# B of two head pairs loaded from ScalarE's and GpSimd's queues instead of SyncE's, with some factor copies moved on ScalarE

## The chip, the cores and the metric

The kernel runs on one core of a Trainium2 chip. The metric is the device time of one execution in microseconds (us). The kernel before takes 122.59 us, the median of three runs (122.33 to 122.97).

## The reference

Two layers follow each other. The first is a scan in chunks (a state-space layer): 4 batches, 8 heads, 768 tokens, head width 32, state width 16. In words: with `cum` the running sum of log(a) inside a chunk,

```
M        = (C @ B.T) * exp(cum_i - cum_j), causal
y        = M @ x + (C @ state) * exp(cum)
state    = exp(sum(la)) * state + (B * exp(cum_last - cum)).T @ x
```

The second is a bilinear feed-forward layer on the heads put side by side (3072 tokens, width 256, inner width 1536): `out = ((y @ w_a) * (y @ w_b)) @ w_out`.

## The kernel before, in words

The sequence is cut into 6 blocks of 128 tokens. A block has two pairs of batches, so there are 12 pairs: pairs 0 and 1 are block 0, pairs 2 and 3 block 1, pairs 4 and 5 block 2. The order of the work is written out by hand: on each engine and on each DMA queue the instructions stand in the order of the program text.

What is computed for a pair:

- **Scaled B and C.** The decay is put on B and C as factors. `batch_factors` (L301) copies the factors from a turned tile `Pt` to `FC`, one copy for each batch, and `batch_inverse` (L309) takes the reciprocal on VectorE to get `FB`. `scale_q` (L341) multiplies C and B of a pair by them on GpSimd into a tile `planes`; its inputs `cq` and `bq` come in four DMAs each for a block (`load_q`, L160, one DMA for each batch). `turn` (L353) transposes `planes` on VectorE, and `scores` (L398) multiplies them on TensorE into the four banks `SC`.
- **Masks.** `mask` (L442) multiplies the scores by the causal table, on VectorE, or by way of a ScalarE copy `tmp` on GpSimd.
- **State.** B is needed a second time with tokens on the partitions, as `bn` (two DMAs for each of the pairs 2 and 3, `load1` at L143, DMA line L153). `scale_bc` (L324, line L333) scales it on GpSimd to `bm`, which `outputs` (L532) multiplies with x. The pairs 2 and 3 take x in fp32 by SyncE (`load_x32`, L721) and ScalarE casts it at L725.
- **Feed-forward.** For block 0 a `unit` (L626) is a pair p and a number k2: `unit_mm` (L593, line L598) makes four matmuls with `Wa` into a bank `aps` and four with `Wb` into a bank `bps`; ScalarE copies `aps` to `asb` (L612), and VectorE multiplies `bps` by `asb` into `hk` (`times`, L622). `out_mm` (L637) multiplies `hk` with `Wo`. From block 1 on, `bunit` (L659, lines L667 and L679) and `bout` (L693, L705) do the same for a whole block.

PSUM has eight banks. Four are the scores' `SC`; the other four are given out in turn by `bank` (L129), which takes the next digit of the string `BANKS`. A matmul that writes a bank waits until its last user has been read. So `BANKS` decides on whom TensorE waits.

Around the change (all in the part that starts at 20 us): the units (0,3), (0,4) and (1,3) are done together: three times `Wa`, three ScalarE copies, then three times `Wb` with `times` behind each on VectorE. `turn(2)` stands on VectorE after `times` of (0,4) and ahead of `times` of (1,3). Then come the unit (0,5), the matmuls of unit (1,4), `scores(2)`, `turn(3)`, the masks of pair 2, unit (1,5), the first halves of `out_mm`, `scores(3)`, the masks of pair 3, `outputs(1)`, and block 1's feed-forward. `turn(4)` and `scores(4)` of block 2 stand after four `bunit`s of block 1.

Each DMA of the queues of SyncE and ScalarE adds to one of eight counters in turn, and an instruction that uses a counter again first waits until the DMA before it on that counter has landed. DMAs of GpSimd's queue have eight counters of their own.

Of the kernel before, what the change touches and what calls it, by code (L numbers as in the profile page):

```python
# [19 lines left out]
SS = 64.0  # L20

BANKS = (
    "012313213212301230123012302103120312301230132013210320132012301230132103210321023013201320"
    "1321023102310231021302130213021302130213021302310231023102310231023102310231023102310"
)


# [1 line left out]
def kernel(  # L29
# [13 lines left out]
    nc = tc.nc  # L43

    nb, H, S, D = x.shape
# [14 lines left out]
    NT = NBLK - PJ // NBP  # L60
# [72 lines left out]
    def tiles(p):  # L133
        Bn = inp.tile([128, H, 2, N], f32, name="bn", tag="bn")
        Cn = inp.tile([128, H, 2, N], f32, name="cn", tag="cn") if p < PJ else None
        X16 = inx.tile([128, H, 2, D], f16, name="xn", tag="xn")
        pair_in[p] = (Bn, Cn, X16)
        st.setdefault(p, {})["X16"] = X16

    def by_token(t_):  # L140
        return t_.rearrange("p h r n -> p (h r n)").rearrange("p (t h n) -> p t h n", t=2, h=H)

    def load1(eng, p, which, bt, i0=0, n=64, to=None):  # L143
        blk, bp = divmod(p, NBP)
        if p >= P2:
            return eng.dma_start(
                by_token(pair_in[p][which])[:, bt],
                (B, C, x)[which][2 * bp + bt, :, blk * Q : (blk + 1) * Q, :].rearrange("h q n -> q h n"),
            )
        src = (B, C, x)[which][2 * bp + bt, :, blk * Q + 2 * i0 : blk * Q + 2 * i0 + 2 * n, :]  # L150
        if to is None:
            to = pair_in[p][which]
        return eng.dma_start(  # L153
            to[64 * bt + i0 : 64 * bt + i0 + n].rearrange("i h r n -> i h (r n)"),
            src.rearrange("h (i r) n -> i h (r n)", r=2),
        )

    ALL_Q = tuple((w, b) for w in (1, 0) for b in range(nb))

    def load_q(eng, blk, parts=ALL_Q):  # L160
        if blk not in by_batch:
            by_batch[blk] = [inq.tile([128, H, 4, N], f32, name=n_, tag=n_) for n_ in ("bq", "cq")]
        return [
            eng.dma_start(  # L164
                by_batch[blk][w][32 * b : 32 * b + 32].rearrange("i h s n -> i h (s n)"),
                (B, C)[w][b, :, blk * Q : (blk + 1) * Q, :].rearrange("h (i s) n -> i h (s n)", s=4),
            )
            for w, b in parts
        ]

    def load2(eng, p, which):
        if p < P2:
            return [load1(eng, p, which, bt) for bt in range(2)]
        blk, bp = divmod(p, NBP)
        src = (B, C, x)[which][2 * bp : 2 * bp + 2, :, blk * Q : (blk + 1) * Q, :]
        return [
            eng.dma_start(  # L177
                by_token(pair_in[p][which]).rearrange("p t h n -> p (t h) n"), src.rearrange("t h q n -> q (t h) n")
            )
        ]  # L180
# [120 lines left out]
    def batch_factors(lo, hi, *bs, eng=None):  # L301
        for b in bs:
            (eng.tensor_copy if eng else nc.scalar.copy)(
                FC[32 * b : 32 * b + 32, lo:hi].rearrange("p k s h -> p (k s) h"),
                Pt[:, lo:hi].rearrange("p k s (b h) -> p (k s) b h", b=nb)[:, :, b],
            )
# [91 lines left out]
    def scores(p):  # L398
        s = st[p] if p < PJ else st["U", p]
        BT, CT = s["BT"], s["CT"]  # L400
        s["T1"] = mid.tile([128, 4, 4, Q], f16, name="t1", tag="t1")

        def score(o_, b_, c_, at):
            nc.tensor.matmul(o_, b_, c_, start=True, stop=True, skip_group_check=True, tile_position=at)  # L404

        if p >= P2:
            for j, b in itertools.product(range(4), range(nb)):
                rows = slice(32 * b, 32 * b + 32)
                score(SC[b][:, j * Q : j * Q + Q], BT[rows, j], CT[rows, j // 2], (32 * b, 0))
            return  # L410
        for e, r, m, bt in itertools.product(range(2), range(2), range(4), range(2)):
            c0 = (e * 2 + r) * Q
            o_ = SC[m][64 * bt : 64 * bt + 64, c0 : c0 + Q]
            if p >= PJ:
                bp, g = divmod(m, 2)
                row = 32 * (2 * bp + bt)
                rows = slice(row, row + 32)
                b_ = BT[rows, 2 * g + e].rearrange("p (i r) -> p r i", r=2)[:, r]
                score(o_, b_, CT[rows, g], (row, 64 * bt))
            else:  # L420
                rows = slice(32 * m, 32 * m + 32)
                score(o_, BT[rows, e, r, bt], CT[rows, bt], (32 * m, 64 * bt))
# [151 lines left out]
    def state_spread(blk):  # L574
        Sbd = mid.tile([128, H // 2, 2 * D], f16, name="spair", tag="spair")
        nc.gpsimd.tensor_tensor(
            out=Sbd.rearrange("p g (e d) -> p (g e) d", e=2),
            in0=V32[:, blk].rearrange("p g (e d) -> p (g e) d", e=2),
            in1=Ge[:, blk].unsqueeze(2).broadcast_to((128, H, D)),
            op=ALU.mult,  # L580
        )
        st["S", blk + 1] = Sbd

    def state_decay(blk):
        if blk + 1 < NG:
            nc.gpsimd.tensor_tensor(
                out=gV[:, blk + 1],
                in0=V32[:, blk],
                in1=G[:, :, blk].unsqueeze(2).broadcast_to((128, H // 2, 2 * D)),
                op=ALU.mult,  # L590
            )

    def unit_mm(p, k2, W):  # L593
        ps = bank("aps" if W is Wa else "bps")
        for kk in range(2):
            k = 2 * k2 + kk
            for f in range(2):
                nc.tensor.matmul(  # L598
                    ps[:, kk * 2 * Q : (kk + 1) * 2 * Q],
                    W[k // 6][:, f, k % 6 // 3 * 384 : (k % 6 // 3 + 1) * 384].rearrange("p (c kk) -> p kk c", kk=3)[  # L600
                        :, k % 3
                    ],
                    X2T[:, p, :, f],
                    start=(f == 0),
                    stop=(f == 1),
                    skip_group_check=True,
                )
        return ps

    def evac_a(a_ps, on_dve=False):  # L610
        asb = ffh.tile([128, 512], f32, name="asb", tag="asb")
        (nc.vector.tensor_copy if on_dve else nc.scalar.copy)(asb, a_ps)  # L612
        return asb

    def times(p, k2, b_ps, asb, by_pool=False):
        s = st[p]
        if "hk" not in s:
            s["hk"] = ffh.tile([128, NK, 2 * Q], f16, name="hk", tag="hk")
        eng = nc.vector
        if by_pool:  # L620
            eng, b_ps = nc.gpsimd, evac_a(b_ps)
        eng.tensor_tensor(  # L622
            out=s["hk"][:, 2 * k2 : 2 * k2 + 2, :].rearrange("p k q -> p (k q)"), in0=b_ps, in1=asb, op=ALU.mult
        )

    def unit(p, k2, between=None, by_pool=False):  # L626
        a_ps = unit_mm(p, k2, Wa)
        if between:
            between()
        b_ps = unit_mm(p, k2, Wb)  # L630
        asb = evac_a(a_ps)
        return lambda: times(p, k2, b_ps, asb, by_pool)
# [78 lines left out]
    def loads_b(*ps):  # L711
        for p in ps:
            if p < NP:
                tiles(p)
                load2(nc.sync, p, 0)
# [30 lines left out]
    def spread(blk):  # L746
        if blk < NBLK - 1:
            state_spread(blk)
            state_decay(blk)
# [67 lines left out]
    for p in (2, 3):  # L817
        tiles(p)
    x_in = [load_x32(p) for p in (2, 3)]
    for p in (2, 3):  # L820
        load2(nc.sync, p, 0)
    warmup(tcp, 512, 512)
    transposes(1, apart=True)
    aps = [unit_mm(0, 0, Wa)]
# [18 lines left out]
    for m in range(3):  # L843
        mask(product(1, m))
    bps = [unit_mm(0, k2, Wb) for k2 in range(3)]
    load_q(nc.sync, 2, ALL_Q[:6])
    loads_b(4, 5)
    times(0, 0, bps[0], asb[0])
    times(0, 1, bps[1], asb[1], by_pool=True)
    gps = fps[:, 96 : 96 + H // 2 * NG]  # L850
# [33 lines left out]
        op=ALU.mult,  # L884
    )
    spread(0)
    late = ((0, 3), (0, 4), (1, 3))
    aps = [unit_mm(p, k2, Wa) for p, k2 in late]
    asb = [evac_a(a_ps) for a_ps in aps]
    batch_factors(2, NT, *range(nb))  # L890
    for (p, k2), a_sb_ in zip(late, asb):
        times(p, k2, unit_mm(p, k2, Wb), a_sb_)
        if k2 == 4:
            turn(2)
    go((0, 5))
    h = unit(1, 4)
    scores(2)
    turn(3)
    mask(product(2, 3), by_pool=True)
# [1 line left out]
    h()  # L901
    h5 = unit(1, 5)
    mask(product(2, 2), by_pool=True)
    load_q(nc.gpsimd, 2, ALL_Q[6:])
    mask(product(2, 1))
    o = [bank("ops"), bank("ops")]
    out_mm(0, 0, o[0], range(6))
    out_mm(0, 1, o[1], range(6))
    batch_factors(1, 2, 0, 1)
    h5()  # L910
    o.append(bank("ops"))
    out_mm(1, 0, o[2], range(6))
    scores(3)
    mask(product(3, 3), by_pool=True)
    batch_factors(1, 2, 2, 3)
    scale_bc(2, 0, nc.gpsimd)
    scale_bc(3, 0, nc.gpsimd)
    nc.gpsimd.memset(causal_q, SS)
# [11 lines left out]
    for c in range(3):  # L930
        p, bt = divmod(c, NBP)
# [136 lines left out]
```

## Time and profile before

| | |
|---|---|
| median of three runs | 122.59 us (122.33 to 122.97) |
| the execution that was profiled | 122.9 us |
| its span, from the first to the last instruction | 121.2 us |
| TensorE matmul (PE) busy | 115.9 us (96%) |
| weight load (PEld) | 75.5 us (62%) |
| VectorE (DVE) | 90.2 us (74%) |
| ScalarE (ACT) | 67.4 us (56%) |
| GpSimd (POOL) | 58.7 us (48%) |
| granted TensorE clock, mean | 0.998 |
| DMA traffic | 12.13 MB, mean 100 GB/s |

A row of the timeline or of the chain has the start in us from the span's start, the time it took, the engine and what it did; rows of the same kind that follow each other are merged, with their number as xN. SPq, ACTq and POOLq are the parts of SyncE, ScalarE and GpSimd that issue DMAs. In brackets stands how long the engine was idle before the row, and what ended that. PE's ends are modelled, so the starts are what counts for it: four matmuls of 256 columns, or two of 512, start 0.43 to 0.45 us after each other.

### The profile page before, as it was taken

The numbers are of one execution on the slowest core, as the hardware profiler recorded it, in microseconds if no ns is written. First come the engines' busy times: TensorE is split into PE (matmuls) and PEld (weight loads), VectorE is DVE, ScalarE is ACT, GpSimd is POOL, SyncE is SP. The second block draws the span as 40 slices with busy tenths as digits, with TensorE's granted clock in tenths as the row PEclk, the third lists the DMA queues.
The fourth block names the chain that finished last, engine by engine and source line by source line (L and its number), as shares of the span: only waits on it lengthen the run. The fifth ranks groups of instructions, "written<-read, shape, count | busy, mean of one in ns | idle before, by whom it ended". The sixth has DMA issues, their size and how long they took to land.

```text
span 121.2 us, 3577 instructions
## 1 busy us (share of the span) xinstructions
PE 115.9 (96%) x1399; PEld 75.5 (62%) x1400; DVE 90.2 (74%) x165; ACT 67.4 (56%) x135; POOL 58.7 (48%) x92
## 2 busy tenths in 40 slices
PE   7989999999999999999999999999999999999990
PEld 5646799788644478644475464775465684645880
DVE  4998889799989995599966999677899426748000
ACT  0446659648567655577566737635735637475230
POOL 7994887997479999386902994200000000000000
PEclk9999999999999999999999999999999999999999
DMA  2999999986769996999992919012001111010131
GB/s 62 135 172 194 205 216 187 206 123 135 113 90 102 145 112 119 102 108 145 200 239 89 86 5 124 7 46 92 0 0 46 44 43 48 0 43 0 49 121 52
DMA packets 59297, 12.13 MB, mean 100 GB/s; under 512 B 54480, under 2 KB 59216, under 8 KB 59280
## 3 DMA queue, kind: packets, MB, share of 16 engines
q0 software_dynamic: 20320, 3.80, 38.3%
q1 hardware_dynamic: 36432, 7.74, 33.8%
q10 hardware_dynamic: 2528, 0.36, 1.8%
q8 instruction: 11, 0.18, 0.7%
q14 instruction: 6, 0.05, 0.1%
HBM read 12.42 MB, written 3.15 MB: 128 GB/s over the span
## 4 chain that ended last, share of the span: by engine, by line
PE 68%; DMA 14%; SPq 10%; POOL 3%; issue 1%; DVE 0%; ACT 0%; POOLq 0%
PE ops L693 22%; PE aps L667 20%; PE bps L667 20%; SPq L153 8%; DMA cq<-in_C_dram 6%; DMA Wa<-in_moe_w_a_dram 5%; DMA bq<-in_B_dram 3%; PE SC L404 2%; SPq L164 2%; PE SC L473 2%; POOL xn L153 1%; PE SC L536 1%; POOL causal L225 1%; POOL planes L346 1%; DVE turned L359 0%
## 5 line engine op out<-in xcount | busy, mean ns | idle before, releaser
L612 ACT COPY asb<-aps 128x512 f32<-128x512 f32 x72 | 41.9, 586 | 15.6 <-PE aps L667 13.3
L679 DVE TENSOR_TENSOR hkb<-bps,asb 128x512 f16<-128x512 f32 x60 | 40.3, 687 | 11.9 <-ACT asb L612 10.5
L667 PE MATMUL aps<-XB,Wa 128*128 128x512 f16 x120 | 35.8, 379 | 0.0
L667 PE MATMUL bps<-XB,Wb 128*128 128x512 f16 x120 | 35.7, 379 | 0.0
L693 PE MATMUL ops<-Wo,hkb 128*128 128x256 f16 (+1 forms) x252 | 28.1, 268 | 0.0
L693 PEld LDWEIGHTS <-hkb 128*128 128x128 f16 x252 | 23.0, 98 | 3.8
L667 PEld LDWEIGHTS <-Wb 128*128 128x128 f16 x120 | 12.4, 103 | 13.5
L667 PEld LDWEIGHTS <-Wa 128*128 128x128 f16 x120 | 12.1, 103 | 11.5 <-issue 0.2
L449 DVE TENSOR_TENSOR t<-SC,causal_q 128x512 f16<-128x512 f32 x27 | 17.3, 682 | 2.4 <-PE SC L404 2.4
L705 ACT ACTIVATE osb<-ops 128x256 f32<-128x256 f32 (+1 forms) x20 | 7.6, 378 | 18.4 <-PE ops L693 18.4
L447 POOL TENSOR_TENSOR t<-tmp,causal_q 128x512 f16<-128x512 f32 x5 | 5.8, 1157 | 8.8 <-ACT tmp L446 8.8
L177 POOL DMA_DIRECT2D xn<-in_x_dram x8 | 9.5, 1190 | 0.0
L346 POOL TENSOR_TENSOR planes<-bq,FB 128x256 f16<-128x256 f32 x10 | 7.5, 770 | 2.0 <-DMA bq<-in_B_dram 1.4
L446 ACT COPY tmp<-SC 128x512 f32<-128x512 f32 x10 | 5.9, 588 | 4.1 <-PE SC L404 3.8
L346 POOL TENSOR_TENSOR planes<-cq,FC 128x256 f16<-128x256 f32 x10 | 7.6, 775 | 0.9 <-DMA cq<-in_C_dram 0.8
L449 DVE TENSOR_TENSOR t<-SC,causal 128x512 f16<-128x512 f32 x11 | 7.0, 681 | 0.7 <-PE SC L404 0.6
L622 DVE TENSOR_TENSOR hk<-bps,asb 128x512 f16<-128x512 f32 x11 | 7.2, 670 | 0.2 <-ACT asb L612 0.2
L598 PE MATMUL aps<-X2T,Wa 128*128 128x256 f16 x48 | 6.8, 274 | 0.0
L558 ACT ACTIVATE XB<-SC 128x512 f16<-128x512 f32 (+1 forms) x9 | 4.6, 548 | 4.1 <-PE SC L501 2.4
L598 PE MATMUL bps<-X2T,Wb 128*128 128x256 f16 x48 | 6.6, 273 | 0.1
L359 DVE STREAM_TRANSPOSE turned<-planes 128x384 f32<-128x384 f32 x10 | 5.5, 564 | 1.1 <-POOL planes L346 1.1
L447 POOL TENSOR_TENSOR t<-tmp,causal 128x512 f16<-128x512 f32 x5 | 5.7, 1154 | 0.3
(101 smaller groups left out, 110.6 us busy)
## 6 DMA issues: line engine op xcount, KB each, us to landing
out_dram<-osb SPq DMA_DIRECT2D x23, 128.0 KB, 1.9
cq<-in_C_dram SPq DMA_DIRECT2D x20, 64.0 KB, 2.7
bq<-in_B_dram SPq DMA_DIRECT2D x18, 64.0 KB, 3.8
bn<-in_B_dram SPq DMA_DIRECT2D x8, 128.0 KB, 3.9
xn<-in_x_dram POOLq DMA_DIRECT2D x8, 128.0 KB, 5.2
Wa<-in_moe_w_a_dram POOLq DMA_DIRECT2D x2, 384.0 KB, 7.4
Wb<-in_moe_w_b_dram POOLq DMA_DIRECT2D x2, 384.0 KB, 8.0
Wo<-in_moe_w_out_dram POOLq DMA_DIRECT2D x2, 384.0 KB, 6.8
```

The lines of the kernel that those rows point to most:

```text
L153: return eng.dma_start(to[64 * bt + i0 : 64 * bt + i0 + n].rearrange("i h r n -> i h (r n)"), src.rearrange("h (i r) n -> i h (r n)", r=2),)
L177: eng.dma_start(by_token(pair_in[p][which]).rearrange("p t h n -> p (t h) n"), src.rearrange("t h q n -> q (t h) n"))
L346: eng.tensor_tensor(out=plane[:, c0 : c0 + 4 * step].rearrange("p (j c) s -> p j s c", c=step)[:, :, :, 0:N], in0=by_batch[blk][which][:, ...
L447: nc.gpsimd.tensor_tensor(out=o_, in0=tmp, in1=c_, op=ALU.mult)
L449: nc.vector.tensor_tensor(out=o_, in0=i_, in1=c_, op=ALU.mult)
L598: nc.tensor.matmul(ps[:, kk * 2 * Q : (kk + 1) * 2 * Q], W[k // 6][:, f, k % 6 // 3 * 384 : (k % 6 // 3 + 1) * 384].rearrange("p (c kk) -> ...
L612: (nc.vector.tensor_copy if on_dve else nc.scalar.copy)(asb, a_ps)
L622: eng.tensor_tensor(out=s["hk"][:, 2 * k2 : 2 * k2 + 2, :].rearrange("p k q -> p (k q)"), in0=b_ps, in1=asb, op=ALU.mult)
L667: nc.tensor.matmul(t_, W[k // 6][:, f, k % 6 // 3 * 384 : (k % 6 // 3 + 1) * 384].rearrange("p (c kk) -> p kk c", kk=3)[:, k % 3], XB[:, b ...
L679: return lambda: nc.vector.tensor_tensor(out=s["hk"][:, k], in0=ps[1], in1=asb, op=ALU.mult)
L693: nc.tensor.matmul(o_ps[:, 0:w], hk[:, k, c * Q : (c + 1) * Q], Wo[:, k, cs], start=(k == 0), stop=(k == NK - 1), skip_group_check=True,)
L705: nc.scalar.activation(out=o_sb[:, 0:w], in_=o_ps[:, 0:w], func=AF.Copy, scale=1.0 / (YS * YS))
```

## The change

- The two DMAs of pair 2's `bn` go from SyncE's queue to ScalarE's, after the three ScalarE copies of `late` and ahead of the factor copies. The two of pair 3's go to GpSimd's queue, after `spread(0)` and ahead of the first masks of pair 2 there.
- SyncE's queue has block 2's `cq` and `bq` directly after the x of the pairs 2 and 3. All eight DMAs are SyncE's; the two that GpSimd issued are gone from it.
- The factor copies on ScalarE: before, four copies for the blocks from 3 on stood after the copies of `late`, and four small ones for block 2 stood later, two behind the masks of pair 2 and two behind that of pair 3. Now two copies do all blocks from 2 on for the batches 0 and 1, two do the blocks from 3 on for the batches 2 and 3, and the two small ones left stand behind the copies of units (0,5) and (1,4).
- `BANKS` is another string from its 27th digit on. On TensorE, VectorE and GpSimd the computing instructions keep their order.

```diff
 BANKS = (
-    "012313213212301230123012302103120312301230132013210320132012301230132103210321023013201320"
-    "1321023102310231021302130213021302130213021302310231023102310231023102310231023102310"
+    "012313213212301230123012301203210321302130231023120310231021302130231203120312013023102310"
+    "2312013201320132012301230123012301230123012301320132013201320132013201320132013201320"
 )
...
     x_in = [load_x32(p) for p in (2, 3)]
-    for p in (2, 3):
-        load2(nc.sync, p, 0)
...
     bps = [unit_mm(0, k2, Wb) for k2 in range(3)]
-    load_q(nc.sync, 2, ALL_Q[:6])
-    loads_b(4, 5)
...
     spread(0)
+    load2(nc.gpsimd, 3, 0)
     late = ((0, 3), (0, 4), (1, 3))
     aps = [unit_mm(p, k2, Wa) for p, k2 in late]
     asb = [evac_a(a_ps) for a_ps in aps]
-    batch_factors(2, NT, *range(nb))
+    load2(nc.scalar, 2, 0)
+    load_q(nc.sync, 2)
+    loads_b(4, 5)
+    batch_factors(1, NT, 0, 1)
+    batch_factors(2, NT, 2, 3)
     for (p, k2), a_sb_ in zip(late, asb):
         times(p, k2, unit_mm(p, k2, Wb), a_sb_)
         if k2 == 4:
             turn(2)
     go((0, 5))
     h = unit(1, 4)
+    batch_factors(1, 2, 2, 3)
     scores(2)
     turn(3)
...
     mask(product(2, 2), by_pool=True)
-    load_q(nc.gpsimd, 2, ALL_Q[6:])
     mask(product(2, 1))
...
-    batch_factors(1, 2, 0, 1)
     h5()
...
     mask(product(3, 3), by_pool=True)
-    batch_factors(1, 2, 2, 3)
     scale_bc(2, 0, nc.gpsimd)
```

## The prediction

> **What bounds the kernel now.** First the page: PE is busy 96% of a span of 121.2 us and the granted clock is 9 tenths or more in all 40 slices, so only gaps in PE's row can be won, and whatever holds PE is lost. Then the chain of work that ended last, in order of time (start, us, what):
>
> ```profile
> 20.17 0.64 SPq L153
> ...
> 24.80 0.63 SPq L153
> ...
> 27.32 0.63 SPq L164
> ...
> 29.97 3.85 DMA bq<-in_B_dram
> 33.82 0.02 issue
> ...
> 33.98 0.78 POOL planes L346
> ...
> 34.78 0.59 DVE turned L359
> 35.37 0.05 issue
> 35.42 0.40 PE SC L404 x16
> ```
>
> Up to 29.97 us it is SyncE issuing one DMA behind another, then the landing of block 2's last B, its scaling on GpSimd, `turn(4)`, and `scores(4)`. From 35.42 us to the end it is PE alone. PE's four `bunit`s before it end with a start at 34.59 us, and a pair of 512-column matmuls takes 0.43 us, so PE was free at 35.02 and waited **0.40 us**. That is all the block 2 path costs: the most that the change can win.
>
> Next the timelines of PE, VectorE and ScalarE around 20 us, where the moved instructions go:
>
> ```profile
> 20.48 0.60 PE L598 MATMUL aps<-X2T,Wa 128*128 128x256 f16 x4
> 20.92 0.60 PE L598 MATMUL bps<-X2T,Wb 128*128 128x256 f16 x4
> 21.36 0.60 PE L598 MATMUL aps<-X2T,Wa 128*128 128x256 f16 x4
> 21.81 0.60 PE L598 MATMUL bps<-X2T,Wb 128*128 128x256 f16 x4
> 22.57 0.65 PE L404 MATMUL SC<-turned 32*64 32x128 f16 x32 [0.16 <-DVE turned L359]
> 23.15 0.62 PE L598 MATMUL aps<-X2T,Wa 128*128 128x256 f16 x4
> ```
> ```profile
> 19.88 1.29 DVE L622 TENSOR_TENSOR hk<-bps,asb 128x512 f16<-128x512 f32 x2
> 21.94 0.58 DVE L359 STREAM_TRANSPOSE turned<-planes 128x384 f32<-128x384 f32 x1 [0.77 <-POOL planes L346]
> 22.44 0.65 DVE L622 TENSOR_TENSOR hk<-bps,asb 128x512 f16<-128x512 f32 x1
> ```
> ```profile
> 18.45 1.56 ACT L612 COPY asb<-aps 128x512 f32<-128x512 f32 x3
> 19.96 1.11 ACT L303 COPY FC<-Pt 32x96 f32<-32x96 f32 x4
> 21.18 0.59 ACT L612 COPY asb<-aps 128x512 f32<-128x512 f32 x1
> 21.99 0.58 ACT L612 COPY asb<-aps 128x512 f32<-128x512 f32 x1 [0.23 <-PE aps L598]
> ```
>
> The PE rows are `aps` and `bps` of unit (0,5), `aps` and `bps` of unit (1,4), `scores(2)`, `aps` of (1,5). The row to watch is 21.81: `bps` of (1,4). Before, `BANKS` gives it bank 2, whose last user, `aps` of (0,5), is copied out by ScalarE from 21.18 to 21.77. It starts 0.04 us later: no slack at all. VectorE does `turn(2)` at 21.94, late because block 1's B landed at about 21.1 (GpSimd scales it at 21.14; the last of the four was issued at 14.67), and only then `times` of (1,3), from 22.44 to 23.09.
>
> **The change part by part.**
>
> *ScalarE's copy of (0,5).* Two DMAs of 64 KB now stand ahead of the factor copies. ScalarE's own rows for such DMAs, at the start of the kernel, are 0.65 and 0.70 us; SyncE's run from 0.63 to 2.34. I take 0.67, because ScalarE's queue is empty at 20 us, as it was in its own rows, while SyncE's long rows stand behind many DMAs of its own. The counters that they wait on belong to block 1's third C (landed about 18.3) and first B (about 19.1): no wait. So DMAs from 19.97 to 21.36, then four copies. A 32x96 copy steps by 0.28, and 32x128 is about 0.03 more (32x32 takes 0.22): 1.17 us, to about 22.55. The copy of (0,5) then runs from 22.5 to 23.1 instead of 21.18 to 21.77, that of (1,4) to 23.6.
>
> *`bps` of (1,4).* With bank 2 it would start at 23.1. The new `BANKS` gives it bank 1, last used by `bps` of (1,3), which VectorE reads in `times` of (1,3), to 23.09. So either way it starts at **23.13 instead of 21.81**. Queued behind it on PE is `scores(2)`, whose input is there at 22.52: it goes from 22.57 to 23.13 + 0.44 = 23.57, **1.00 us later**. All of PE's work follows in order.
>
> *What of that is absorbed.* Nothing before 35 us. `aps` of (1,5) would start at 24.15 (its bank is free at 23.1). VectorE's `times` of (0,5) is only 0.1 late, and its masks of pair 2 end about 26.05, before PE asks for these banks at 26.92 + 0.15. The later stages (masks of pair 3, `outputs(1)`, the first `bunit`s) move by the same 1.00 us. PE's short gaps behind `out_mm` (25.98 to 26.14) occur again at later changes from `ops` to `SC`, so they aren't slack.
>
> *SyncE's queue.* Four DMAs of B (5.75 us of issue, 21.52 to 27.27) are gone. Block 2's C does not simply start at 21.52, though. Its third and fourth DMAs wait on the counters of the first two x, which landed 5.3 and 7.3 us after issue (22.9 and 25.6), and its last B on that of the last x (20.85 + 5.8 = 26.6). At 0.45 a piece, the last B goes out at 27.1 at the latest, 2.9 us before 29.97, and lands by 31 with the before's 3.85. GpSimd gets to it after `causal_q`, at about 31.3.
>
> *GpSimd.* Two issues of B are added; its own rows at L153 (x, 64 KB) are 0.69 to 0.87, so 1.45 us from 23.86, and two of 0.61 are removed. Its first mask moves from 23.97 to 25.4 and the second ends at 27.7; PE needs them in `outputs(1)`, at 30.7 now. Its third mask waits for `scores(3)` and moves with PE. Hidden; without that cover it would be 0.2 us net. B of pair 3 has from 25.4 to 30.2 to land (5.6 is the median for early loads, 2.5 for the two it issued at 26).
>
> *`scores(4)`.* PE is now free at 36.02. The scaled planes are ready by about 33, VectorE does `turn(4)` right behind its second product, 35.40 to 35.98, and PE goes on at 36.02: the wait of **0.40 us is gone**. Late is then the product before it, with no loss. The four moved small copies cost nothing: ScalarE waited 1.67 us before its mask copy at 26.88.
>
> *One more term.* The new DMAs on ScalarE's queue start at 20 us, while block 1's last B is landing until 21.1, and that landing leads to `turn(2)` and `times` of (1,3). The windows view has the DMA engines fully busy there (share 1.25 from 20 to 21 us, packets overlapping). Bounds: 0, and 0.5 (the last 1.1 us shared among three queues instead of two: half as much again). I take 0.1, as the first of ScalarE's data can come only after an issue of 0.67.
>
> The Trainium skill (DMA: Bandwidth & Descriptors, "Issuing engines are not separate DMA queues") holds that DMAs from all issuing engines run on the same 16 DMA engines, so that another issuer saves only issue time. The trace bears that out in part: SyncE's four B cost 5.75 us of issue and land in 3.9 to 5.7 us. By that rule the upper bound of this term is the likelier, and the sum would be +1.1; by the empty queue it is +0.6.
>
> **Sum:** +1.00 - 0.40 + 0.1 = **+0.7 us**. The profiled execution took 122.9 (span 121.2), so 123.6 by it; it lay 0.3 above the median, and I add to the median: 122.59 + 0.7 = **123.3**. About 0.5% (0.6 us) is what a measurement of this kernel can tell from no change, so this is just slower.
>
> **The rivals.**
>
> - *ScalarE's issue stalls like SyncE's.* For it: SyncE's second x took 1.84 us at 18.28, and two of its four B 2.34 and 1.80. Against: the empty queue. With one such row the copy of (0,5) ends at 24.3, `aps` of (1,5) starts 0.15 late and the bank of the second `out_mm`, behind the copy of (1,5), costs 0.35 more: 123.8. With both, at 2.34 and 1.80, that copy ends at 25.9 and `aps` of (1,5) starts 1.8 late: 125.0. In between: 124.2. Chance 0.20.
> - *Block 1's B lands late because of the shared DMA engines,* the bound of 0.5: 123.7. In the trace a loaded queue needs about 6 us for a DMA that takes 2.5 us unloaded. Chance 0.10.
> - *Not slower: block 1's B lands earlier.* The hold on `bps` of (1,4) ends with `times` of (1,3), and that hangs on this landing alone as long as VectorE waits for it (0.77 us). If it lands 0.77 earlier than in this execution, `times` of (1,3) ends at 22.32, `scores(2)` starts at 22.8, PE is free for `scores(4)` at 35.25, and the sum is -0.15: 122.4. It decides from 0.6 earlier on. Against it: nothing ahead of 20 us changes. For it: the landing (6.0 to 6.4 us after issue) is the most variable thing there, and ScalarE must then be done in time too. Chance 0.14.
> - *The change does not do what it says:* SyncE still waits for landings of x, as above. It costs nothing, since `scores(4)` has 2 us to spare once PE is late. It is part of the forecast.
>
> **How the numbers follow.** Forecast 0.50 (123.1 to 123.5; two thirds of it beyond 0.5%), ScalarE's stall 0.20, late B 0.10, early B 0.14, anything else 0.06. Slower: 0.33 + 0.20 + 0.10 = 0.63. Same: 0.17 + 0.13 + 0.02 = 0.32. Faster by over 0.5%: 0.05, as the trace shows only 0.40 us to win. The range reaches down to the early B, 122.3, and up past the middle of ScalarE's stall, 124.4; the double stall is left out.
>
> **What would show it.** In the changed profile: PE idle of about 1.3 us before `bps` of unit (1,4), ended by VectorE's L622; `scores(2)` near 23.6; no wait before `scores(4)`, near 36.1; ScalarE's two issues near 20 us at about 0.67 each; SyncE's last `bq` of block 2 before 28. I am wrong if `bps` of (1,4) starts before 22.5, if an issue on ScalarE takes over 1 us, or if PE makes up the 1.0 us between 24 and 35.

## The result, and the profile after

The changed kernel takes **123.18 us**, the median of 21 runs (122.58 to 124.31), against 122.55 us for the kernel before in the same session (21 runs, 122.06 to 123.26). The ratio is **1.0056, 95% interval 1.0033 to 1.0079**: slower, by about 0.6 us, and 0.12 us from the forecast of 123.3.

The execution profiled for the changed kernel took 122.72 us (span 121.0), among its fastest. TensorE's timeline in it, first around `bps` of unit (1,4) (rows: `aps` of (1,4), `bps` of (1,4), `scores(2)`), then around `scores(4)` (last row):

```profile
21.22 0.60 PE L598 MATMUL aps<-X2T,Wa 128*128 128x256 f16 x4
22.22 0.60 PE L598 MATMUL bps<-X2T,Wb 128*128 128x256 f16 x4 [0.40 <-DVE hk L622]
22.75 0.65 PE L404 MATMUL SC<-turned 32*64 32x128 f16 x32
...
34.72 0.59 PE L667 MATMUL bps<-XB,Wb 128*128 128x512 f16 x2
35.25 0.40 PE L404 MATMUL SC<-turned 32*128 32x128 f16 x16
```

VectorE and ScalarE there:

```profile
21.01 0.58 DVE L359 STREAM_TRANSPOSE turned<-planes 128x384 f32<-128x384 f32 x1
21.51 0.65 DVE L622 TENSOR_TENSOR hk<-bps,asb 128x512 f16<-128x512 f32 x1
```
```profile
19.25 0.60 ACTq L153 DMA_DIRECT2D bn<-in_B_dram  x1
19.32 0.60 ACT L612 COPY asb<-aps 128x512 f32<-128x512 f32 x1
19.89 0.65 ACTq L153 DMA_DIRECT2D bn<-in_B_dram  x1
20.58 1.17 ACT L303 COPY FC<-Pt 32x128 f32<-32x128 f32 x4 [0.65 <-DVE hk L622]
21.77 1.07 ACT L612 COPY asb<-aps 128x512 f32<-128x512 f32 x2
```

Starts are what to read on PE. The step from 21.22 to 22.22 is 1.00 us, against 0.45 in the profile of before (21.36 to 21.81): PE was held for 0.55 us, and the bracket names VectorE's `times` as what ended it. On VectorE `turn(2)` (21.01) needed no wait for block 1's B in this execution, and still stands ahead of `times` of (1,3), which ends at 22.16. The step from the last `bunit` to `scores(4)` is 0.53 us. ScalarE's bracket (0.65) names a wrong releaser: the factor copies don't read `hk`, and without the two DMAs (run t4_no_b2 below) they start at 20.13, when the product has only begun. The engine's queue was issuing the second DMA until 20.54.

This execution is the prediction's rival "block 1's B lands earlier" nearly word for word: 22.8 and 35.25 were given for `scores(2)` and `scores(4)`. But the rival set that early B in the changed kernel against a late B in the kernel before, and so found no loss. It is 0.18 us below the profiled execution of before, while the medians differ by 0.63 the other way. So one profile of each kernel does not explain the result, and each was profiled once more.

### The profile page after: what moved, and what is told of

It is laid out like the page before. It is cut to its first block, busy times and chain, and to the rows that moved or that the text cites. A ratio compares the mean times of both kernels' runs of the same rounds, so it can differ in the third digit from the quotient of the medians.

```text
span 121.0 us, 3576 instructions
## 1 busy us (share of the span) xinstructions
PE 115.9 (96%) x1400; PEld 75.6 (62%) x1400; DVE 90.3 (75%) x165; ACT 67.3 (56%) x133; POOL 58.8 (49%) x92
## 4 chain that ended last, share of the span: by engine, by line
PE 93%; DVE 3%; issue 1%; ACT 0%; DVEq 0%
PE ops L693 22%; PE aps L667 22%; PE bps L667 21%; PE bps L598 5%; PE ops L637 5%; PE aps L598 4%; PE SC L404 4%; PE SC L238 3%; PE SC L473 2%; DVE t L449 1%; PE SC L536 1%; PE tc L238 1%; PE py L458 1%; PE SC L485 1%; DVE hk L622 1%
## 5 line engine op out<-in xcount | busy, mean ns | idle before, releaser
L622 DVE TENSOR_TENSOR hk<-bps,asb 128x512 f16<-128x512 f32 x11 | 7.3, 669 | 0.5 <-ACT asb L612 0.5
L637 PE MATMUL ops<-Wo,hk 128*128 128x256 f16 x48 | 5.8, 273 | 0.0
```

The costliest lines, as they stand in the source:

```text
L622: eng.tensor_tensor(out=s["hk"][:, 2 * k2 : 2 * k2 + 2, :].rearrange("p k q -> p (k q)"), in0=b_ps, in1=asb, op=ALU.mult)
L637: nc.tensor.matmul(o_ps[:, 0:d_model], hk[:, k, bt * Q : (bt + 1) * Q], Wo[:, k, :], start=(k == 0), stop=(k == NK - 1), skip_group_check= ...
```

## The experiments

All kernels were timed in several rounds against the kernel before. The first four shared 33 runs of it (median 122.55), the next four 32 (122.58), the last three 29 (122.6). "Step" is the time from the start of `aps` to the start of `bps` of (1,4) in the profiled execution, 0.45 without a hold. "Last step" is the time from the last matmul pair of the `bunit`s to `scores(4)`, 0.53 without a wait. "Stretch" is the time from the start of `aps` of (1,4) to the start of `scores(4)`; where PE waits for nothing in it, it is 13.34 (second profile of before). From `scores(4)` to the start of ScalarE's last copy of the output all 13 profiles take 82.51 us, with the old `BANKS` and with the new: the rest of the string costs nothing there.

| kernel | median us | ratio (95%) | step | last step | stretch |
|---|---|---|---|---|---|
| before (first profile) | 122.55 | 1 | 0.45 | 0.83 | 14.06 |
| after | 123.18 | 1.0056 (1.0033 to 1.0079) | 1.00 | 0.53 | 14.03 |
| t1_turn_later | 123.08 | 1.0038 (1.0015 to 1.0060) | 0.46 | 0.52 | 13.86 |
| t2_banks_only | 123.29 | 1.0060 (1.0034 to 1.0085) | 1.02 | 0.53 | 14.16 |
| t3_no_b_wait | 122.99 | 1.0046 (1.0021 to 1.0070) | 1.06 | 0.53 | 14.20 |
| t4_no_b2 | 123.29 | 1.0058 (1.0034 to 1.0082) | 0.94 | 0.53 | 14.04 |
| t7_turn_no_b3 | 122.70 | 1.0018 (0.9997 to 1.0040) | 0.47 | 0.53 | 13.73 |
| t8_b3_sync | 123.01 | 1.0035 (1.0004 to 1.0065) | 0.47 | 0.53 | 13.52 |
| t5_old_banks | 123.10 | 1.0055 (1.0023 to 1.0087) | 1.39 | 0.53 | 14.27 |
| c1_before_again | 122.35 | 0.9996 (0.9973 to 1.0018) | 0.46 | 0.53 | 13.34 |
| t9_no_scalar_dma | 122.85 | 1.0015 (0.9992 to 1.0038) | 0.47 | 0.53 | 13.57 |
| t10_own_queue | 122.81 | 1.0008 (0.9987 to 1.0029) | 0.45 | 0.53 | 13.56 |
| c2_after_again | 123.29 | 1.0056 (1.0033 to 1.0079) | 1.73 | 0.53 | 14.61 |

**Both kernels again.** Builds with nothing changed but a comment line at the end, for a second time and profile of each.

> The kernel before once more, as another build: ratio 1.000, within 0.998 to 1.002, by every theory here. If it comes out beyond 1.003, differences of this size between builds can't be put down to an edit.

> The changed kernel once more, as another build: ratio 1.003 to 1.008 as before by every theory here. Its profile tells how large the hold on bps of (1,4) is in a second execution: 0.4 to 0.6 us longer than the 0.44 us of a matmul pair if block 1's B lands early, up to 1.0 us longer if it lands late; scores(4) without a wait in both cases.

The differences between kernels repeat: 0.9996 and 1.0056. TensorE in the second profile of before (122.30 us):

```profile
21.47 0.60 PE L598 MATMUL aps<-X2T,Wa 128*128 128x256 f16 x4
21.93 0.60 PE L598 MATMUL bps<-X2T,Wb 128*128 128x256 f16 x4
22.46 0.65 PE L404 MATMUL SC<-turned 32*64 32x128 f16 x32
...
34.28 0.59 PE L667 MATMUL bps<-XB,Wb 128*128 128x512 f16 x2
34.81 0.40 PE L404 MATMUL SC<-turned 32*128 32x128 f16 x16
```

There is no wait before `scores(4)` at all: the step is the 0.53 us of every other kernel here. The one that the change was to take away is thus not in every execution of before. Where it is, it is smaller than the 0.40 us that the prediction read; its row in the first profile, in the timeline with idle times, says 0.24, and 0.83 less 0.53 is 0.30:

```profile
35.42 0.40 PE L404 MATMUL SC<-turned 32*128 32x128 f16 x16 [0.24 <-DVE turned L359]
```

TensorE and VectorE in the second profile of after (123.72 us):

```profile
21.65 0.60 PE L598 MATMUL aps<-X2T,Wa 128*128 128x256 f16 x4
23.38 0.60 PE L598 MATMUL bps<-X2T,Wb 128*128 128x256 f16 x4 [1.13 <-DVE hk L622]
23.91 0.65 PE L404 MATMUL SC<-turned 32*64 32x128 f16 x32
...
36.26 0.40 PE L404 MATMUL SC<-turned 32*128 32x128 f16 x16
```
```profile
22.17 0.58 DVE L359 STREAM_TRANSPOSE turned<-planes 128x384 f32<-128x384 f32 x1 [0.71 <-POOL planes L346]
22.68 1.25 DVE L622 TENSOR_TENSOR hk<-bps,asb 128x512 f16<-128x512 f32 x2
```

This is the forecast itself (a hold of about 1.3 us, `scores(2)` near 23.6, `scores(4)` near 36.1), 0.29 us later throughout, as `aps` of (1,4) is: here block 1's B is late, VectorE waits 0.71 us in front of `turn(2)`, `times` of (1,3) stands behind it, and PE is held by 1.28 us (1.73 less 0.45), more than the "up to 1.0 us" expected for this run.

So there is an early and a late case of each kernel, and the change costs something in both. From `aps` of (1,4) to `scores(2)` it is 0.99 us in before and 1.53 in after where B is early, 1.21 and 2.26 where it is late: 0.54 and 1.05 us more.

**The BANKS alone.** The kernel before with only the new `BANKS`:

```diff
 BANKS = (
-    "012313213212301230123012302103120312301230132013210320132012301230132103210321023013201320"
-    "1321023102310231021302130213021302130213021302310231023102310231023102310231023102310"
+    "012313213212301230123012301203210321302130231023120310231021302130231203120312013023102310"
+    "2312013201320132012301230123012301230123012301320132013201320132013201320132013201320"
 )
```

> The kernel before with the new BANKS alone, all DMAs and copies as before. Theory: bps of unit (1,4) is held until the product of (1,3) is done, about 1.0 us, of which the wait of 0.40 us before scores(4) absorbs 0.4: ratio about 1.005 (1.003 to 1.007). Rival (the moved DMAs are what costs): ratio 1.000.

1.0060: the whole loss, without one DMA or copy moved. PE is held by VectorE's L622 as in after (step 1.02). That no bank further down the string adds to it is shown by the 82.51 us behind `scores(4)`.

**The old BANKS in the changed kernel**, the reverse edit:

> The changed kernel with the BANKS of before. The matmul bps of unit (1,4) then waits for ScalarE's copy of (0,5), which stands behind two DMA issues and four factor copies and ended at 22.36 us in the profile after: a hold of about 0.7 us against 21.66, whatever block 1's B does. Theory (either bank is held, so BANKS and the moved copies are one cause in two places): ratio 1.004 to 1.007. Rival (the new BANKS alone carry the loss): ratio 0.997 to 1.000.

1.0055. PE is held as well (0.94 us, expected 0.7), now by ScalarE's copy of (0,5), which stands behind the two DMAs and the four factor copies:

```profile
23.68 0.60 PE L598 MATMUL bps<-X2T,Wb 128*128 128x256 f16 x4 [0.79 <-ACT asb L612]
```

So the two parts of the change exclude each other's cure: with the moved instructions on ScalarE the old bank is late, and the new bank is late by itself.

**Block 1's B never late.** In the changed kernel block 1's scaled B is made from the tile of C, which lands earlier; the values of B in block 1 are left out.

```diff
-            in0=by_batch[blk][which][:, 4 * u : 4 * u + 4],
+            in0=by_batch[blk][1 if blk == 1 else which][:, 4 * u : 4 * u + 4],
```

> The changed kernel where block 1's scaled B is made from its C tile, so that nothing waits for the landing of block 1's B (the values of B in block 1 are left out). Theory: turn(2) runs at about 21 us, the product of (1,3) ends by 22.2, the hold is 0.4 us, scores(2) starts near 22.7; 0.1 to 0.3 us under the kernel before (ratio about 0.998), and the times scatter less than those of the changed kernel. Rival (ScalarE's copy of unit (0,5), late behind its DMAs, or GpSimd's issues are the cost): the time of the changed kernel, ratio about 1.005.

The expected 0.998 was missed: 1.0046. VectorE shows why. Block 1's B is not waited for, and the hold is still 0.61 us (PE from 21.24 to 22.30), since `turn(2)` and `times` of (1,3) take 1.15 us one behind the other:

```profile
21.09 0.58 DVE L359 STREAM_TRANSPOSE turned<-planes 128x384 f32<-128x384 f32 x1
21.59 0.65 DVE L622 TENSOR_TENSOR hk<-bps,asb 128x512 f16<-128x512 f32 x1
```

Nor do the times scatter less, as was expected: 1.05 us from lowest to highest, against 0.87 in c2_after_again.

**ScalarE without the two DMAs.** In the changed kernel pair 2's B isn't loaded a second time; its scaling reads pair 3's tile.

```diff
-    load2(nc.scalar, 2, 0)
```

> The changed kernel without pair 2's second load of B: the two DMAs on ScalarE's queue are gone, and pair 2's bm is made from pair 3's tile (pair 2's own B is left out there). Theory: the hold is VectorE's and stays, so the time is that of the changed kernel, ratio 1.003 to 1.007, though ScalarE's copy of (0,5) comes 1.3 us earlier. Rival (the two DMAs on ScalarE cost, by their issue or by holding up the landing of block 1's B): 0.998 to 1.001.

1.0058, and a step of 0.94: the two issues on ScalarE aren't what costs while VectorE holds the bank, nor do their transfers make block 1's B late. In the late execution of after, the last of block 1's four B was issued at 15.32 and landed at 21.12, against 14.14 and 19.74 in the early one: most of the delay was there at its issue, 4 us ahead of ScalarE's first DMA (19.67).

**`turn(2)` behind the three products** in the changed kernel, so that `times` of (1,3) is not queued behind it:

```diff
     for (p, k2), a_sb_ in zip(late, asb):
         times(p, k2, unit_mm(p, k2, Wb), a_sb_)
-        if k2 == 4:
-            turn(2)
+    turn(2)
```

> The changed kernel with turn(2) behind the product of unit (1,3) on VectorE instead of ahead of it. Theory (the loss is the hold of bps of unit (1,4), whose bank is read by that product, which stands behind turn(2), which waits for block 1's B): bps of (1,4) starts by 22.0 us without a hold, scores(2) starts within 0.2 us of turn(2)'s end, no wait before scores(4), and the time is 0.2 to 0.5 us under the kernel before (ratio about 0.997), so 0.8 to 1.2 us under the changed kernel. Rival (the loss comes from the DMAs issued by ScalarE and GpSimd): no better than the changed kernel, ratio 1.004 or more.

The hold is gone (step 0.46), but most of the loss stayed: 1.0038 instead of 0.997, which by the time alone is nearer to the rival; against the rival stand t2 and t4. In this profile other waits have come up, 0.52 us in the stretch against c1: 0.13 at `out_mm` behind `scores(2)`, and 0.39 at the matmuls `ds` (L512, `bm` with x), which take 0.90 us instead of 0.51. These wait for pair 3's B, which GpSimd's queue brings 6.3 us after issue; GpSimd waits for it and PE's weight load for GpSimd. GpSimd's row and PE's:

```profile
30.64 0.62 POOL L333 TENSOR_TENSOR bm<-bn,fB 128x256 f16<-128x256 f32 x1 [0.85 <-DMA bn<-in_B_dram]
```
```profile
31.32 0.28 PEld L512 LDWEIGHTS <-bm 64*32 64x32 f16 x16 [0.25 <-POOL bm L333]
```

Another 0.80 us was lost in this execution at 10 us, ahead of everything that was changed, to a late landing of pair 1's B; the profile of t2 has the same, and neither profile of after. It is scatter and belongs to no edit.

**Without GpSimd's load, or with it on SyncE.** Both have `turn(2)` behind the products. In the first (t7) pair 3's second half is scaled from pair 2's tile and `load2(nc.gpsimd, 3, 0)` is left out. In the second (t8):

```diff
-    load2(nc.gpsimd, 3, 0)
...
     load2(nc.scalar, 2, 0)
+    load2(nc.sync, 3, 0)
     load_q(nc.sync, 2)
```

> The changed kernel with turn(2) behind all three products, and without the second load of pair 3's B: its second half is scaled from pair 2's tile (so the values of B in pair 3 are wrong, the work is the same). With turn(2) behind the products alone the ratio was 1.0038, and its profile showed 0.25 us of PE time lost where GpSimd scales pair 3's B late. If that late landing on GpSimd's queue is what is left: 0.2 to 0.3 us less, ratio 1.000 to 1.002. If GpSimd's two DMAs cost nothing (rival: the rest is the later scores(2), still at about 23.0 us against 22.57): ratio as without this edit, 1.003 to 1.005.

> The changed kernel with turn(2) behind all three products, and pair 3's B loaded by SyncE between its x and block 2's loads; ScalarE keeps pair 2's B. If late landing on GpSimd's queue is what is left of the loss: pair 3's B lands by about 27 us, before GpSimd's turn to scale it, and the ratio is 0.997 to 1.001 (hold gone, no wait before scores(4)). If SyncE's two issues put block 2 late again, the wait before scores(4) is back with up to 0.4 us. If neither queue matters: 1.003 to 1.005.

1.0018 and 1.0035, with intervals that overlap each other's and t1's: the first is what was expected if the late landing was what was left, the second what was expected if neither queue mattered. The wait of PE for GpSimd is gone in both profiles, but the times don't tell for sure what it cost. In t7 the next late thing shows: `out_mm` waits for ScalarE's copy of (1,5), behind the DMAs (the second took 0.91 us there).

```profile
25.00 1.47 PE L637 MATMUL ops<-Wo,hk 128*128 128x256 f16 x12 [0.23 <-ACT asb L612]
```

**ScalarE's DMAs out as well.** t8 without `load2(nc.scalar, 2, 0)`, as in t4, and a version that computes everything: the changed kernel with the old `BANKS`, pair 2's B on SyncE, and pair 3's on GpSimd, issued right behind block 1's scaling:

```diff
     scale_q(3, 0, nc.gpsimd)
+    load2(nc.gpsimd, 3, 0)
     state_sums(0)
...
-    load2(nc.gpsimd, 3, 0)
...
-    load2(nc.scalar, 2, 0)
+    load2(nc.sync, 2, 0)
     load_q(nc.sync, 2)
```

> The kernel with turn(2) behind the products and pair 3's B on SyncE, and now without ScalarE's load of pair 2's B: its second half is scaled from pair 3's tile (the values of B in pair 2 are wrong, the work is the same). Theory: with the hold on bps of (1,4) gone, the next to come late is ScalarE, whose two DMA issues delay the copies behind them (out_mm waited 0.23 us for the copy of (1,5) in one profile). Then VectorE's wait of 0.3 us for the copy of (0,5) and the waits of out_mm go, scores(2) starts within 0.15 us of the 12.35 us ahead of scores(4) that the profile of the kernel before again shows, and the ratio is 0.998 to 1.001. Rival (ScalarE's issues have slack, the rest is scatter or BANKS): ratio as without this edit, 1.002 to 1.005.

> The changed kernel with the BANKS of before, pair 2's B on SyncE between its x and block 2, and pair 3's B on GpSimd right behind the scaling of block 1, so that ScalarE's queue has no DMA there. Theory: bps of (1,4) waits only for ScalarE's copy of (0,5), which ends at about 21.8 us as before: no hold, no wait before scores(4), ratio 0.997 to 1.000. If GpSimd's load still lands later than 29.5 us: up to 0.3 us more, 1.000 to 1.002. If the gain of the change is nothing in most executions (the wait before scores(4) was 0.40 us in one profile of before and 0.10 us, the bare change of bank, in another): not under 0.998.

1.0015 and 1.0008: no difference from before that these runs can tell, though both lie above what was expected with no wait left (up to 1.001 and 1.000). With none of the moved DMAs on ScalarE's queue and no hold, the loss is gone, and no gain has taken its place. So no version here beats the kernel before. The profiled execution of t10 was its longest (124.37 us): PE stood idle for 1.30 us, up to 14.31, for the load of a weight `Wb`, ahead of the change.

In the profiles of t4, t9 and t10 something else has come up: PE waits 0.22 us ahead of the third `bps` of block 1's feed-forward (a step of 0.66 us in t10 instead of 0.43).

```profile
34.75 0.59 PE L667 MATMUL aps<-XB,Wa 128*128 128x512 f16 x2
35.41 0.59 PE L667 MATMUL bps<-XB,Wb 128*128 128x512 f16 x2
```

It waits for a product of VectorE, and that for ScalarE's first copy `asb` there, which starts 1.02 us after the start of its matmuls in these three and 0.69 in the profile of after and the second of before. What holds that copy the trace doesn't say; it is all that the stretches of t9 and t10 have above 13.34.

## Why the prediction was right, and where not

- **The mechanism was right.** `bps` of (1,4) is held on bank 1 until VectorE's `times` of (1,3), which is queued behind `turn(2)`: after, t2, t3, t4 and the second profile of after all show it; t1, t7, t8 and t9 show it gone with `turn(2)` moved. t2 shows that it is enough for the whole loss; that removing it alone gives all of it back is not shown (t1). That "with bank 2" it would be late too is shown by t5 (hold 0.94 us).
- **The term of +1.00 us is one for the late case.** As the delay of `scores(2)` it measured 1.05 us late against late and 0.54 early against early. The prediction knew the early case (`times` of (1,3) ending at 22.32, a hold of 0.55), but called it "not slower", for it set it against the one late profile of before. t3 shows that the hold stays, at 0.6 us, when B isn't waited for at all.
- **The term of -0.40 us was mis-sized.** 0.10 us of it is the step that PE takes from a `bunit` to `scores(4)` in every profile; the rest, 0.30 us, is there in one of two profiles of before. The chain of waits of one execution gave the prize as if it were paid in each.
- **The sum.** Half-way between the two profiles of each kernel: `scores(2)` later by 0.80, wait shorter by 0.15, so +0.65 us, an estimate from two executions each; measured 0.0056 x 122.55 = 0.69. The forecast of +0.7 is right partly by luck: +1.00 was 0.20 too much, -0.40 took off 0.25 too much, and the 0.1 wasn't there.
- **The term of +0.1 us** (ScalarE's transfers delay block 1's B) isn't seen: without them (t4) the hold and the ratio are those of after, and most of B's delay was there before they were issued. The upper bound of 0.5, and with it the sum of +1.1 us, was not borne out.
- **ScalarE's copy of (0,5)** was put at 22.5 to 23.1 and ended near 22.36. The two DMAs took 0.60 and 0.65 us, as taken (0.67), but the first was issued at 19.25, beside the third copy, not after it. The rival of stalled issues fell: the longest in any profile here was 0.91 us, not 2.34.
- **SyncE's block 2** was said to be out before 28 us; the last issue ended at 28.6 and 29.2 in the two profiles of after (the eight issues took 7.7 us in the first; 0.45 a piece had been taken), and GpSimd scaled block 2 without a wait. The wait before `scores(4)` is gone in every changed kernel, as said.
- **GpSimd's load of pair 3's B** was called hidden, though the prediction's own figures left it 4.8 us (25.4 to 30.2) and gave 5.6 as the median of a landing. In the first profile of after GpSimd waited 0.61 us for it and `ds` took 0.15 us longer; in the second, where PE is later, it is hidden. The queue alone is not to blame: with that load on SyncE, GpSimd waited 0.61 us in the first profile of before and 0.72 in t2, and the prediction overlooked this wait in its profile.
- **Adding the sum to the median** and not to the profiled execution was right: that execution (122.9) held waits that others don't have, and the kernel before again had a median of 122.55. By the same reasoning the -0.40 had no place in full in a sum on the median.

Left open: how often block 1's B is late. Two profiles of after show one case each; a kernel of before with B never late was not tried. The 0.2 to 0.4% left in t1, t7 and t8 is split by one profile each (t1 as above; 0.39 and 0.17 us at `out_mm` in t7 and t8), but the medians don't follow these amounts, so what is scatter stays open.

## What to carry to other kernels

A wait that one profile shows is a price in that execution; before it is counted as a prize, take a second profile and look whether it is there, and take off the step that PE makes at that place anyway. An early or late landing is to be set into both kernels, not into the changed one alone. When the order in which banks are handed out changes, follow the bank back to its last reader and read what stands ahead of that reader on its engine: a matmul that had no slack was moved here from a ScalarE copy to a VectorE product behind a transpose, which cost 0.55 us without anything late. And when a hold is taken away, expect the next late thing to show (here a load on GpSimd's queue and copies behind ScalarE's DMAs) before the time comes back.

## What the runs showed of the hardware

- ScalarE's DMA issue ran beside its own compute: in after the first stands at 19.25 for 0.60 us, while the copy ahead of it in the program runs from 19.32 to 19.92. What stands behind the DMAs did wait: the factor copies started at 20.58, after the second issue's end at 20.54. All seven profiles with these DMAs show both, with 0.04 or 0.05 us from the second issue's end to the first factor copy.
- Another queue did not make a load land earlier. The DMA groups from 12 to 32 us (columns: transfer, queue, count, KB each, median us from issue to landing), of after and of before again:

```profile
bn<-in_B_dram ACTq DMA_DIRECT2D x2, 64.0 KB, 6.3
bn<-in_B_dram POOLq DMA_DIRECT2D x2, 64.0 KB, 6.3
```
```profile
bn<-in_B_dram SPq DMA_DIRECT2D x4, 64.0 KB, 5.1
```

  These are 6.3 us on the two new queues against 5.1 on SyncE's. Over the 13 profiles the medians for such loads overlap: 4.7 to 7.2 us on SyncE's queue, 4.7 to 6.8 on GpSimd's and 6.3 to 7.5 on ScalarE's.

  The Trainium skill (DMA: Bandwidth & Descriptors, "Issuing engines are not separate DMA queues") has DMAs of all issuing engines share the same 16 DMA engines, so that another issuer saves only issue time. The landings here agree with it: neither of the two new queues brought its loads earlier than SyncE's.
- Landings scatter by about a microsecond between executions of one kernel: with `aps` of (1,4) at 21.22 and 21.65, block 1's last B landed at 19.74 and 21.12 in the two profiles of after, that is 0.95 us later when the shift of 0.43 is taken off, and VectorE's `turn(2)` came at 21.01 and 22.17, 0.73 us later. That is more than the whole difference of the two kernels.
